# Folding a spectrum about its middle column before the back transform: two narrower matmuls out of three, 32 more vector operations

## The chip, the cores and the metric

The kernel runs on one core of a Trainium2 chip. The core has a matrix engine (PE, TensorE), a vector engine (DVE, VectorE), a scalar engine (ACT, ScalarE), a general engine (POOL, GpSimd) and a queue engine (SP, SyncE) that issues most transfers. Each engine takes its own instructions in order; semaphores tie them together. PE writes its results to PSUM, eight banks of 512 float32 columns, and DVE or ACT copy them from there.

The metric is the device time of one execution in microseconds (us).

## The reference, cut to what matters

Two mixers of the same input x (2048 tokens, 640 features) are blended by a gate:

```python
g = sigmoid((x * gate_w).sum(-1, keepdims=True))
a = _A_ref(x, A_wq, A_wk, A_wv, A_wo, A_beta)   # 32 heads, 4 causal segments of 512, with a memory between segments
b = _B_ref(x, B_w_r, B_w_i)
return g * a + (1 - g) * b

def _B_ref(x, w_r, w_i):
    X = rfft2(x.astype(float32), axes=(-2, -1))   # tokens and features
    X = X * (w_r + 1j * w_i)                      # one filter of 2048 x 321
    return irfft2(X, s=(S, D), axes=(-2, -1)).astype(bfloat16)
```

Only the second mixer, b, is touched. Its last step turns 321 complex columns k of the spectrum into 640 real features d. With real part Yr and imaginary part Yi (already back in tokens), feature d is a sum over k of Yr[k] cos(2 pi k d / 640) minus Yi[k] sin(2 pi k d / 640). The cosine part is even about d = 320 and the sine part is odd, so features d and 640 - d come from the sum and the difference of the two parts, each computed for d = 0 to 320 only.

## The kernel before, in words

**The attention** works through four segments. The logits of a segment are made in 20 units (qk_unit, L1283), 80 units in all. A unit is a group of small matmuls into four PSUM banks, an exponential on ACT (L1319) and causal masks on POOL (L1340). Products with the values, projections, feature maps on DVE (L1140, L1141) and a running memory (mem, L1193 to L1216) go with it. Segments 0 to 2 send their unnormalised outputs through DRAM (u_scr, r_scr, o_scr) and read them back for the output projection (finish_tile, L1563).

**The spectral mixer** is written in `fft` (L1422). Everything is bf16 in SBUF.

- x is folded about the middle feature on DVE or POOL (L956, L961): sums and differences with one operand read backwards, so that the forward feature transform needs narrower tables.
- F1: matmuls transform 128-token blocks and put features on the partitions (Ac).
- Sixteen groups g follow. D: six matmuls per group against tables in `big`, of 160, 161 and 321 columns, give 321 columns of cosine and of sine terms, copied to Bt (L571 on ACT or L573 on DVE). T: four matmuls with twiddle tables (tt) complete the token transform. W_mul (L1496, DVE): the filter. W_add (L1501, DVE or POOL): real and imaginary part of the filtered spectrum, written to Yt, which has two buffers. Tb: six matmuls per group with Yt as the weights, in chunks of 128, 128 and 65 columns; they put the column k on the partitions, and their results are copied to Cp.
- Db follows when all sixteen groups are in Cp. For each of 16 token blocks n2 and for cosine and sine (typ), three matmuls, one per chunk of k, add up 321 columns in one bank: 96 matmuls. The cosine part is copied to eo (ACT or DVE), and two operations on DVE (sum_Db, L1542) add and subtract it with the sine part in PSUM and write features 0 to 319 in order and 639 to 320 backwards to G. G is later read by the final matmuls (Fb) under the gate.

**The order of the work** is written out by hand as one tuple of numbers, ORDER (L633). Number // 2 is the operation in the order of recording, and the remainder picks the engine where an operation has two. `either` (L582) gives an operation to DVE or POOL in this way, and `copy_alts` (L567) to ACT or DVE. A pass over the tuple (`schedule`, L117) makes one instruction queue per engine and chooses PSUM banks; `emit` (L290) turns dependences into semaphore waits. An operation that `either` creates is marked with a lock: POOL's next instruction is made to wait for it if it runs on DVE.

Lines that the prediction uses: L561 issues nearly all matmuls (L559 those split into four), L571 and L573 the copies.

Of the kernel before, what the change touches and what calls it, by code (L numbers as in the profile page):

```python
# [8 lines left out]
ALU = mybir.AluOpType  # L9
# [3 lines left out]
P = 128  # L13
S = 2048
D = 640
# [335 lines left out]
def make_tables():  # L351
# [34 lines left out]
    IC = np.zeros((384, 322))  # L386
    IS = np.zeros((384, 322))
    IC[:KD, :KD] = ck[:, None] * np.cos(2 * pi * kd[:, None] * dd[None] / D)
    IS[:KD, :KD] = ck[:, None] * np.sin(2 * pi * kd[:, None] * dd[None] / D)
    IS[0] = 0  # L390
    IS[320] = 0
    IS[:, 320] = 0

# [34 lines left out]
    def chunks(t):  # L428
        return np.ascontiguousarray(t.reshape(3, 128, -1).transpose(1, 0, 2))
    fcat = np.concatenate([F, np.eye(128), Fp], 1)  # L430
    inv = np.concatenate([chunks(IC), chunks(IS)], 1).reshape(128, 6 * 322)
    big = np.concatenate([dtab, inv], 1)
    hmask = np.zeros((128, 5, 8, VW))
    for t in range(5):
        for r in range(128):
# [4 lines left out]
            "hmask": hmask.reshape(128, 880).astype(b)}  # L440

# [63 lines left out]
class Kern:  # L505
# [10 lines left out]
    def b(self, *key):  # L516
        v = self.bufs.get(key)
        if v is None:
            v = self.bufs[key] = Buf(str(key))
        return v  # L520
# [69 lines left out]
    def dma(self, dst, src, nbytes, r, w, prio, tr=False, name="", after=(), queue="sp"):  # L590
# [1073 lines left out]
```

## Time and profile before

| | us |
|---|---|
| median of the three runs | 240.84 (240.61 to 243.23) |
| the profiled execution's own time | 243.11 |
| its span, first to last instruction | 241.1 |
| matmuls reading Cp, first to last start | 166.0 to 204.3 |
| copies to Cp, first to last start | 61.0 to 164.0 |
| W_add, first to last start | 56.2 to 161.2 |

The profile is of one execution, 2.0 us longer than its span, and 2.3 us above the median. The clock granted to PE is 1.00 over the span. A row of a group shows the engine, the operation, what is written and read with shapes, the number of instructions, their busy time in us and the mean of one in ns; then the idle time of the engine just before them and what ended it. The durations of neighbours overlap, so means times counts can exceed the busy time. The chain is the run of work that ended last, followed back from the end.

### The profile page before, as it was taken

How to read it: one execution, taken by the hardware profiler on the slowest of the kernel's cores; microseconds unless marked ns; L12 is line 12 of the kernel's file. 1: busy time of each engine (PE TensorE's matmuls, PEld its weight loads, DVE VectorE, ACT ScalarE, POOL GpSimd, SP SyncE). 2: the span in 40 equal slices, each digit the busy share in tenths (PEclk: the TensorE clock that was granted, in tenths of full speed). 3: DMA queues.
4: the chain of work that ended last, by engine and by line, in shares of the span. 5: the costliest groups of instructions: out<-in, count | busy, mean ns of one | idle time of the engine just before them, and what ended most of it. 6: DMA issues, size and time to landing. Idle time of an engine off the chain costs nothing.

```text
span 241.1 us, 10285 instructions
## 1 busy us (share of the span) xinstructions
PE 225.2 (93%) x4347; PEld 140.6 (58%) x4361; DVE 194.7 (81%) x488; ACT 199.3 (83%) x238; POOL 158.5 (66%) x293
## 2 busy tenths in 40 slices
PE   7999996999999999999899999998998799989994
PEld 2584564776556675544566554455544466746794
DVE  0589796888999987999998999897999878645353
ACT  2199886899999999999999789998999878866830
POOL 8022137647768958648988978967995576767930
PEclk9999999999999999999999999999999999999999
DMA  7999998996978797495864882464668655842224
GB/s 167 276 358 151 277 155 182 243 229 183 225 183 183 204 204 216 100 212 132 231 207 140 225 223 44 154 193 106 200 170 239 189 147 145 113 63 75 71 73 109
DMA packets 59121, 42.18 MB, mean 175 GB/s; under 512 B 30212, under 2 KB 55364, under 8 KB 59076
## 3 DMA queue, kind: packets, MB, share of 16 engines
q1 hardware_dynamic: 57380, 40.71, 69.4%
q10 hardware_dynamic: 1696, 0.82, 1.3%
q8 instruction: 34, 0.56, 0.9%
q14 instruction: 11, 0.09, 0.1%
HBM read 23.32 MB, written 12.30 MB: 148 GB/s over the span
## 4 chain that ended last, share of the span: by engine, by line
PE 52%; DVE 18%; DMA 10%; ACT 9%; POOL 4%; SPq 3%; issue 3%; DVEq 0%
PE psum L561 50%; ACT ex L1319 6%; POOL ex L1340 3%; DVE Pt L1496 3%; DMA mT<-o_scr 3%; SPq L596 2%; PE psum L559 2%; DMA u_scr<-ub 2%; DVE Bt L573 2%; DMA dnc<-u_scr 2%; DVE G L1542 1%; DMA xsb<-in_A_x_dram 1%; DMA r<-r_scr 1%; DVE xf L956 1%; ACT et L1128 1%
## 5 line engine op out<-in xcount | busy, mean ns | idle before, releaser
L1319 ACT ACTIVATE ex<-psum 128x2048 bf16<-128x2048 f32 (+4 forms) x92 | 138.5, 1506 | 16.0 <-PE psum L561 14.4
L1340 POOL TENSOR_SCALAR_AFFINE_SELECT ex<-ex 128x256 bf16<-128x256 bf16 (+2 forms) x224 | 118.8, 553 | 28.8 <-ACT ex L1319 4.4
L561 PE MATMUL psum<-qkp 20*64 20x64 bf16 (+5 forms) x1280 | 32.7, 270 | 5.4 <-DMA qkp<-qk_scr 2.0
L561 PE MATMUL psum<-xT,wk 128*128 128x256 bf16 (+1 forms) x280 | 31.2, 273 | 0.1
L561 PE MATMUL psum<-wv,xT 128*32 128x320 bf16 (+3 forms) x400 | 29.2, 301 | 0.4 <-DVE Bt L573 0.4
L561 PE MATMUL psum<-xT,wq 128*128 128x512 bf16 (+1 forms) x121 | 27.4, 394 | 1.0 <-issue 0.5
L561 PEld LDWEIGHTS psum<-qkp 20*64 20x64 bf16 x1280 | 13.4, 103 | 22.5 <-ACT ex L1319 14.0
L1496 DVE TENSOR_TENSOR Pt<-psum,Wt 128x642 bf16<-128x642 f32 x32 | 25.2, 818 | 0.9 <-PE psum L561 0.8
L561 PEld LDWEIGHTS psum<-xT,wk 128*128 128x128 bf16 (+1 forms) x280 | 20.4, 98 | 6.0 <-issue 1.4
L559 PE MATMUL psum<-wo,oU 128*32 128x320 bf16 x480 | 21.7, 300 | 0.0
L961 POOL TENSOR_TENSOR xsb<-xf 128x320 bf16<-128x320 bf16 (+2 forms) x6 | 4.5, 745 | 24.5 <-DVE phk L1140 11.1
L561 PEld LDWEIGHTS psum<-wv,xT 128*32 128x32 bf16 (+1 forms) x400 | 14.5, 96 | 7.7 <-issue 2.2
L1171 DVE TENSOR_TENSOR va<-psum,ebx 128x320 bf16<-128x320 f32 x32 | 15.2, 485 | 4.7 <-PE psum L561 4.2
L561 PE MATMUL psum<-big,Cp 128*128 128x321 bf16 (+1 forms) x96 | 17.8, 302 | 1.1 <-DVE ot L573 0.7
L573 DVE CAST ot<-psum 128x320 bf16<-128x320 f32 x22 | 10.4, 490 | 9.8 <-PE psum L559 7.0
L561 PE MATMUL psum<-big,Ac 128*128 128x321 bf16 (+2 forms) x96 | 18.2, 257 | 0.1
L561 PE MATMUL psum<-ex,va 128*32 128x64 bf16 (+3 forms) x576 | 17.6, 257 | 0.7 <-DVE mem L1216 0.4
L561 PE MATMUL psum<-tt,Yt 128*128 128x256 bf16 (+1 forms) x96 | 17.0, 276 | 0.5 <-DVE va L1171 0.2
L561 PEld LDWEIGHTS psum<-ex,va 128*32 128x32 bf16 x576 | 10.8, 96 | 10.1 <-POOL ex L1340 2.5
L1542 DVE TENSOR_TENSOR G<-eo,psum 128x320 bf16<-128x320 f32 x32 | 14.9, 477 | 1.3 <-PE psum L561 1.1
L1501 POOL TENSOR_TENSOR Yt<-Pt 128x321 bf16<-128x321 bf16 x17 | 12.4, 731 | 5.3 <-DVE phq L1140 2.4
L1128 ACT ACTIVATE et<-qu 128x512 bf16<-128x512 bf16 x25 | 15.2, 625 | 0.3 <-DVE qu L573 0.2
(98 smaller groups left out, 388.1 us busy)
## 6 DMA issues: line engine op xcount, KB each, us to landing
qkp<-qk_scr SPq DMA_DIRECT2D x28, 160.0 KB
tt<-tab_tt SPq DMA_DIRECT2D x8, 512.0 KB, 4.0
qk_scr<-qu SPq DMA_DIRECT2D x12, 256.0 KB, 3.2
u_scr<-ub SPq DMA_DIRECT2D x12, 256.0 KB, 3.7
xsb<-in_A_x_dram SPq DMA_DIRECT2D x8, 320.0 KB, 6.8
oU<-u_scr SPq DMA_DIRECT2D x15, 128.0 KB, 4.3
out_dram<-ot SPq DMA_DIRECT2D x12, 160.0 KB
Wt<-in_B_w_r_dram SPq DMA_DIRECT2D x16, 80.2 KB, 2.8
```

Of the source, the lines that this page charges most:

```text
L559: h = e.matmul(dst, wt, r_, start=st, stop=sp_, **{**kw, "tile_position": (0, q), "skip_group_check": True})
L561: h = e.matmul(o_, l_, r_, start=st, stop=sp_, **kw)
L573: alts["dve"] = (lambda e: e.tensor_copy(dst(), src()), 67 + 1.04 * n, 68.0)
L596: return e.dma_start(d_, s_)
L961: self.either(lambda e, dst=dst, src=src, d0=d0, n=n, op=op: e.tensor_tensor(xs.ap(o + dst, [D, 2], [1, n]), xf.ap(src + d0, [321, 2], [1, ...
L1128: self.one("act", lambda e: e.activation(et.ap(0, [1, L]), qsl(), ACT.Exp), L, [qb], [b("et", pi_)], late, fix=95, name="phi_exp")
L1171: self.one("dve", lambda e: e.tensor_tensor(va.ap(i * H * VW + h0 * VW, [VW, nh], [1, DH]), self.ps(bank, 0, [DH, nh], [1, DH]), self.ebx. ...
L1319: self.one("act", lambda e, d=d, q=q: e.activation(self.ex.ap(*d), self.ps(bank, *q), ACT.Exp, scale=SC), n, [bank], [self.exb(s, 2 * pr + ...
L1340: self.one("pool", lambda e: e.affine_select(self.ex.ap(e0 + d0, [1280, 4], [1, n], np_=np_), self.ex.ap(e0 + s0, [1280, 4], [1, n], np_=np_),
L1496: self.one("dve", lambda e, ri=ri, Pt=Pt, Wt=Wt, wo_=wo_, bank=bank: e.tensor_tensor(Pt.ap(ri * 322, [644, 2], [1, KD]), self.ps(bank, 0, ...
L1501: fn = lambda e, r=r, a0=a0, a1=a1, op=op, Pt=Pt, Yt=Yt: e.tensor_tensor(Yt.ap(r * 322, [1, KD]), Pt.ap(a0 * 322, [1, KD]), Pt.ap(a1 * 322 ...
L1542: self.one("dve", lambda e, q=q, n2=n2, bank=bank, eo=eo: e.tensor_tensor(self.G.ap(n2 * D + 639 * q, [1 - 2 * q, 320]), eo.ap(q, [1, 320] ...
```

## The change

Column 320 - k has the cosine of column k up to a sign: cos(2 pi (320 - k) d / 640) = (-1)^d cos(2 pi k d / 640), and likewise for the sine with the sign reversed. So even features need only the sums, and odd features only the differences (for the sine the other way round), of columns k and 320 - k.

- **Z_fold** (new, two per group, 32 in all): Zt takes the sums of Yt[k] and Yt[320 - k] for k = 0 to 160 and the differences for k = 0 to 159, real and imaginary part in one operation. It runs on DVE or POOL as ORDER says.
- Tb reads Zt in place of Yt, in the same chunks of 128, 128 and 65.
- Db: the first chunk holds only sums, the last only differences, so they need only the columns of one parity of d. The three matmuls of a bank are 161, 321 and 160 columns wide for the cosine and 160, 321 and 161 for the sine; before, all were 321. The results stand in the bank with the even and the odd features apart.
- sum_Db reads the two halves and writes every second element of G, again in two operations.
- Yt has one buffer, Zt two. The tables in `big` shrink from 3220 to 2576 columns, and so does their load.
- ORDER is another tuple. The 80 logit units come in the same sequence as before. Z_fold is on DVE 22 times and on POOL 10 times; W_add is on DVE 28 times and on POOL 4 times, before 15 and 17.

```diff
-        self.big = T("big", [P, 1288 + 6 * 322])
+        self.big = T("big", [P, 2576])
...
-        self.Yt = [T(f"Yt{i}", [P, 2 * 322]) for i in range(2)]
+        self.Yt = T("Yt", [P, 2 * 322])
+        self.Zt = [T(f"Zt{i}", [P, 2 * 322]) for i in range(2)]
...
+DB_PARTS = (((0, 0, 161, 0), (1, 0, KD, 162), (2, 161, 160, 484)), ((0, 161, 160, 644), (1, 0, KD, 804), (2, 0, 161, 1126)))
...
+            for q, (n, op) in enumerate(((161, ALU.add), (160, ALU.subtract))):
+                self.either(lambda e, q=q, n=n, op=op, Yt=Yt, Zt=Zt: e.tensor_tensor(
+                    Zt.ap(161 * q, [322, 2], [1, n]), Yt.ap(0, [322, 2], [1, n]), Yt.ap(320, [322, 2], [-1, n]), op), 2 * n,
+                    Yb, [b("Zt", g % 2, q)], prio2, after=self.after_q0(("Zt", g % 2, q)), name="Z_fold")
...
-                            return (self.ps(bank, (c % 2) * 256, [1, 256], np_=kc), Yt.ap(r * 322 + c * P, [1, kc]), tt.ap(to + 512 + r * 256, [1, 256]),
+                            return (self.ps(bank, (c % 2) * 256, [1, 256], np_=kc), Zt.ap(r * 322 + c * P, [1, kc]), tt.ap(to + 512 + r * 256, [1, 256]),
...
-                for c in range(3):
-                    kc = 65 if c == 2 else P
-
-                    def th(c=c, typ=typ, kc=kc, n2=n2, bank=bank):
-                        return (self.ps(bank, 0, [1, KD]), self.Cp.ap(c * 4096 + typ * 2048 + n2 * P, [1, P], np_=kc),
-                                big.ap(1288 + (typ * 3 + c) * 322, [1, KD], np_=kc), c == 0, c == 2, {})
+                for n_, (c, c0, n, tc) in enumerate(DB_PARTS[typ]):
+                    def th(c=c, c0=c0, n=n, tc=tc, n_=n_, typ=typ, kc=65 if c == 2 else P, n2=n2, bank=bank):
+                        return (self.ps(bank, c0, [1, n]), self.Cp.ap(c * 4096 + typ * 2048 + n2 * P, [1, P], np_=kc),
+                                big.ap(1288 + tc, [1, n], np_=kc), n_ == 0, n_ == 2, {"skip_group_check": True})
...
-                        self.G.ap(n2 * D + 639 * q, [1 - 2 * q, 320]), eo.ap(q, [1, 320]), self.ps(bank, q, [1, 320]),
+                        self.G.ap(n2 * D + 638 * q, [1, 2], [2 - 4 * q, 160]), eo.ap(q, [161 - q, 2], [1, 160]), self.ps(bank, q, [161 - q, 2], [1, 160]),
                         ALU.subtract if q else ALU.add), 320, [bank, eb], [b("G", n2, q)], prio, name="sum_Db", after=acb)
```

More of the change, by code (lines that the diff above doesn't have):

```diff
@@ L385, in make_tables, with folded @@
     dd = np.arange(KD)
[L386 to L389, printed above, removed]
+    IC = ck[:, None] * np.cos(2 * pi * kd[:, None] * kd[None] / D)
+    IS = ck[:, None] * np.sin(2 * pi * kd[:, None] * kd[None] / D)
+    IC[160] *= 0.5
+    IS[160] *= 0.5
     IS[0] = 0
-    IS[320] = 0
     IS[:, 320] = 0
+    def folded(M, odd):
+        Z = np.zeros((KD, KD))
+        Z[:161, 161 if odd else 0:KD if odd else 161] = M[:161, odd::2]
+        Z[161:, 0 if odd else 161:161 if odd else KD] = M[:160, 1 - odd::2]
+        return Z
+    ZC, ZS = folded(IC, 0), folded(IS, 1)
     T = np.zeros((16, 128, 4, 128))
@@ L426, in make_tables, with part @@
                     putp(0, 0, eo, c), putp(1, 0, eo, -s), putp(0, 1, eo, -s), putp(1, 1, eo, -c)
-    def chunks(t):
-        return np.ascontiguousarray(t.reshape(3, 128, -1).transpose(1, 0, 2))
+    def part(Z, c, c0, c1):
+        q = np.zeros((128, (c1 - c0 + 1) // 2 * 2))
+        rows = Z[128 * c:128 * c + 128, c0:c1]
+        q[:len(rows), :c1 - c0] = rows
+        return q
     fcat = np.concatenate([F, np.eye(128), Fp], 1)
-    inv = np.concatenate([chunks(IC), chunks(IS)], 1).reshape(128, 6 * 322)
+    inv = np.concatenate([part((ZC, ZS)[typ], c, c0, c0 + n) for typ in range(2) for c, c0, n, _ in DB_PARTS[typ]], 1)
     big = np.concatenate([dtab, inv], 1)
@@ L837, in after_mid @@
         return ([b("tt", i) for i in range(self.NT)] + [b("Wt", i, r, h) for i in range(2) for r in range(2) for h in range(2)] +
-                [b("Bt", i, r) for i in range(2) for r in range(2)] + [b("Yt", i, r) for i in range(2) for r in range(2)] +
+                [b("Bt", i, r) for i in range(2) for r in range(2)] + [b("Yt", r) for r in range(2)] + [b("Zt", i, q) for i in range(2) for q in range(2)] +
                 [b("Pt", i, r, q) for i in range(2) for r in range(2) for q in range(2)])
@@ L909, in loads @@
                      P * 2 * D * 2, [], [self.b("xsb", q)], 1.0 + 0.2 * q, name="ld_x")
-        self.dma(lambda: self.big.ap(0, [1, 3220]), lambda: dap(self.tab["big"].ap(), 0, [3220, P], [1, 3220]),
-                 P * 6440, [], [self.b("big")], 5.0, name="ld_big")
+        self.dma(lambda: self.big.ap(0, [1, 2576]), lambda: dap(self.tab["big"].ap(), 0, [2576, P], [1, 2576]),
+                 P * 5152, [], [self.b("big")], 5.0, name="ld_big")
         self.dma(lambda: self.hm.ap(0, [1, 880]), lambda: dap(self.tab["hmask"].ap(), 0, [880, P], [1, 880]),
@@ L1483, in fft @@
                            r=[bank], w=[Bb], after=self.after_q0(("Bt", g % 2, typ)), prio=prio, name="ev_D")
-            Pt, Yt = self.Pt[g % 2], self.Yt[g % 2]
+            Pt, Yt, Zt = self.Pt[g % 2], self.Yt, self.Zt[g % 2]
             Pb = [[b("Pt", g % 2, ri, r) for r in range(2)] for ri in range(2)]
-            Yb = [b("Yt", g % 2, i) for i in range(2)]
+            Yb = [b("Yt", i) for i in range(2)]
             for ri in range(2):
@@ L1502, in fft @@
                     Yt.ap(r * 322, [1, KD]), Pt.ap(a0 * 322, [1, KD]), Pt.ap(a1 * 322, [1, KD]), op)
-                self.either(fn, KD, [Pb[0][r], Pb[1][1 - r]], [Yb[r]], prio2, after=self.after_q0(("Yt", g % 2, r)), name="W_add")
+                self.either(fn, KD, [Pb[0][r], Pb[1][1 - r]], [Yb[r]], prio2, after=self.after_q0(("Yt", r)), name="W_add")
+            for q, (n, op) in enumerate(((161, ALU.add), (160, ALU.subtract))):
+                self.either(lambda e, q=q, n=n, op=op, Yt=Yt, Zt=Zt: e.tensor_tensor(
+                    Zt.ap(161 * q, [322, 2], [1, n]), Yt.ap(0, [322, 2], [1, n]), Yt.ap(320, [322, 2], [-1, n]), op), 2 * n,
+                    Yb, [b("Zt", g % 2, q)], prio2, after=self.after_q0(("Zt", g % 2, q)), name="Z_fold")
+            Zb = [b("Zt", g % 2, q) for q in range(2)]
             for cs in ((0, 1), (2,)):
@@ L1511, in fft, with th @@
                     for r in range(2):
-                        def th(c=c, r=r, kc=kc, Yt=Yt, tt=tt, to=to, bank=bank):
-                            return (self.ps(bank, (c % 2) * 256, [1, 256], np_=kc), Yt.ap(r * 322 + c * P, [1, kc]), tt.ap(to + 512 + r * 256, [1, 256]),
+                        def th(c=c, r=r, kc=kc, Zt=Zt, tt=tt, to=to, bank=bank):
+                            return (self.ps(bank, (c % 2) * 256, [1, 256], np_=kc), Zt.ap(r * 322 + c * P, [1, kc]), tt.ap(to + 512 + r * 256, [1, 256]),
                                     r == 0, r == 1, {})
                         items.append((th, 256))
-                    self.mms(items, Yb + [b("tt", ti), bank], [], prio3, name="Tb", mode=0)
+                    self.mms(items, Zb + [b("tt", ti), bank], [], prio3, name="Tb", mode=0)
                 n_, np_, c0 = len(cs), (65 if cs[0] == 2 else P), cs[0]
@@ L1527, in fft @@
                 bank = Bank(1, "gen")
-                for c in range(3):
-                    kc = 65 if c == 2 else P
-                    def th(c=c, typ=typ, kc=kc, n2=n2, bank=bank):
-                        return (self.ps(bank, 0, [1, KD]), self.Cp.ap(c * 4096 + typ * 2048 + n2 * P, [1, P], np_=kc),
-                                big.ap(1288 + (typ * 3 + c) * 322, [1, KD], np_=kc), c == 0, c == 2, {})
-                    self.mms([(th, KD)], cpb + [b("big"), bank], [], prio, name="Db", mode=0)
+                for n_, (c, c0, n, tc) in enumerate(DB_PARTS[typ]):
+                    def th(c=c, c0=c0, n=n, tc=tc, n_=n_, typ=typ, kc=65 if c == 2 else P, n2=n2, bank=bank):
+                        return (self.ps(bank, c0, [1, n]), self.Cp.ap(c * 4096 + typ * 2048 + n2 * P, [1, P], np_=kc),
+                                big.ap(1288 + tc, [1, n], np_=kc), n_ == 0, n_ == 2, {"skip_group_check": True})
+                    self.mms([(th, n)], cpb + [b("big"), bank], [], prio, name="Db", mode=0)
                 eo, eb = self.eo[n2 % 3], b("eo", n2 % 3)
```

197 rows, old and new, of the table ORDER are left out of this document.

## The prediction

> **What bounds the kernel now.** I read the engine totals first, then the same engines by stretch of the span, then the groups of the rows that the change touches, then the waits and the chain.
>
> ```profile
> PE 225.2 (93%) x4347; PEld 140.6 (58%) x4361; DVE 194.7 (81%) x488; ACT 199.3 (83%) x238; POOL 158.5 (66%) x293
> ```
>
> By the totals TensorE (PE) is the bound and the change takes work from it. But a total is an average over stages, so I cut the span at the exponentials of the logit units (ACT, L1319): the 10th starts at 53.05 us, the 55th at 163.49 us and the 60th at 174.20 us. Busy us of each engine in these stretches:
>
> ```profile
> core 0: us, PE busy (x) PEld busy (x) DVE busy (x) ACT busy (x) POOL busy (x), PEclk, DMA share, GB/s
> ...
> 52.60:163.00 110.40, 106.60 (x1874) 63.52 (x1885) 102.93 (x248) 103.90 (x114) 85.96 (x164) 1.00 0.71 181
> 163.00:173.70 10.70, 9.75 (x200) 6.17 (x192) 9.05 (x27) 9.69 (x12) 8.58 (x19) 1.00 0.59 161
> ...
> 173.70:241.10 67.40, 60.34 (x1569) 40.27 (x1568) 45.54 (x117) 47.82 (x56) 43.59 (x76) 1.00 0.51 126
> ```
>
> In the middle stretch three engines are nearly full together: PE 97%, DVE 93%, ACT 94%. All spectrum groups (L1470 to L1520) run there, and the added instructions go there. The back transform (Db, the matmuls that read Cp) runs from 166.0 to 204.3 us, almost all in the last stretch, where DVE is 68% busy. So the change takes from PE late and gives to DVE in the middle.
>
> [...]
>
> The groups of the rows that change or resemble what is added (busy us, mean ns of one, idle before):
>
> ```profile
> L561 PE MATMUL psum<-big,Cp 128*128 128x321 bf16 x64 | 13.8, 303 | 1.1 <-DVE ot L573 0.7 <-DVE mem L1216 0.2
> L561 PE MATMUL psum<-big,Ac 128*128 128x321 bf16 x32 | 9.4, 302 | 0.0
> L561 PE MATMUL psum<-big,Ac 128*128 128x161 bf16 x32 | 7.4, 235 | 0.1
> L561 PE MATMUL psum<-big,Ac 128*128 128x160 bf16 x32 | 7.3, 234 | 0.0
> L1501 POOL TENSOR_TENSOR Yt<-Pt 128x321 bf16<-128x321 bf16 x17 | 12.4, 731 | 5.3 <-DVE phq L1140 2.4 <-DVE phq L1141 0.9 <-DVE dn L1208 0.7
> L1501 DVE TENSOR_TENSOR Yt<-Pt 128x321 bf16<-128x321 bf16 x15 | 5.4, 374 | 0.1
> L961 DVE TENSOR_TENSOR xsb<-xf 128x322 bf16<-128x322 bf16 x7 | 2.3, 325 | 0.0
> ```
>
> **The change part by part.**
>
> *Removed from PE.* Of each three Db matmuls of 321 columns, two become 160 or 161 columns wide. The forward matmuls from Ac have exactly these widths: 302 ns against 235 and 234, so 67.5 ns less each. 64 such matmuls: **4.3 us less on PE**. The instructions stay 96, the weight loads too. Before 173.7 us the new order does 30 Db matmuls where the old did 27, and keeps 6 more Tb matmuls for that stretch, so nothing is gained there. After it, 69 become 66: about 3.4 us less of PE's 60.3. In the middle stretch PE has the same matmuls but for 2 more D and 6 fewer Tb: nothing.
>
> *Added to DVE and POOL.* 32 Z_fold operations (16 groups, sum and difference, 322 and 320 elements). The written order puts 22 on DVE and 10 on POOL. The same order moves W_add: from 15 on DVE and 17 on POOL to 28 and 4. The fold's nearest row is the fold of x (L961): two bf16 inputs, one read backwards, an odd offset, 322 elements: 325 ns on DVE, and 730 ns for its like on POOL. In the middle stretch (same logit units in both orders) DVE gets 20 Z_fold x 325 = 6.5 and 13 W_add x 374 = 4.9, and loses three copies to Bt (518 each, 1.6), one phi pair (0.8), one copy to Cp (0.7) and three small gate operations (0.5), and gains one projection copy (0.7): **8.5 us more by durations**. Durations of neighbours overlap: in the chain three folds in a row took 0.80 us, 0.27 each, not 0.33. Over the stretch the old order's DVE durations by these rows sum to 117 us and show as 102.9 busy, a factor 0.88. So 7.5 us more, 110.4 us of DVE in a stretch that lasts 110.4. It can only keep its length if DVE never waits. How full can DVE get? Its five fullest ten-microsecond windows in this stretch show 9.87, 9.67, 9.57, 9.55 and 9.54, mean 96.4%; at that, the stretch takes 114.5 us, **4.1 longer**. Bounds: the fullest window's 98.7% gives 111.9 (1.5 longer), today's 93.2% gives 118.4 (8.0 longer). I take the mean of the fullest windows, since PE and ACT get no new work and stop being what DVE waits for. From 163.0 to 173.7 us DVE gets 1.8 us more by the same rows, with 1.65 us of idle: **0.5 longer** (0 to 1.5).
>
> *POOL* loses 13 x 731 = 9.5 and gains 10 x 740 = 7.4: 2 us less, with 24 us idle in the stretch: nothing.
>
> *The last stretch.* Which part of the 3.4 us counts? The chain there:
>
> ```profile
> 80 pieces in order of time: start us, us, what
> ...
> 182.25 4.47 DMA u_scr<-ub
> ...
> 186.74 3.74 DMA dnc<-u_scr
> ...
> 206.27 6.15 DMA mT<-o_scr
> ...
> 228.03 9.62 PE psum L561 x276
> ```
>
> From 182 to 219 us it runs mostly through DMAs, DVE and the masks on POOL, and after 206 us no Db is left. PE holds about 4.5 us of the chain between 174 and 206. Bounds: 0 and 3.4; I take **1.5 shorter**, since some other PE work can slip forward into the freed time. The sums of G (L1542) now write every second element. The copy to Bt writes so too and takes 518 ns for 322 elements where ot takes 490 for 320; 32 x 28 ns = 0.9 us on an engine that is 68% busy: nothing, 0.9 if the cover is gone.
>
> *Small edits.* Yt has one buffer instead of two: the next W_add waits for both folds. Groups come 110/16 = 6.9 us apart, so nothing; it costs up to 0.7 us where the order has two groups close together. One more link (0.33 on DVE, 0.74 on POOL) lies between W_add and Tb; at the end the last Cp copy starts at 164.0 and the first Db at 166.0, which hides it. The table load shrinks by a fifth; it is issued at 42.7 and first read at 51.5 us: nothing. SP issues the same number of transfers.
>
> *Sum.* 4.1 + 0.5 - 1.5 = **3.1 us longer**. The profiled execution took 243.11 us (span 241.1 and 2.0 around it) and would become 246.2. It is 2.3 above the median of 240.84, so on the median's scale I predict **243.9 us**. Extremes: 1.5 + 0 - 3.4 = -1.9 and 8.0 + 1.5 + 0.9 + 0.7 = +11.1.
>
> **Rivals.**
>
> *PE is the bound throughout, DVE has slack (faster).* For it: 97% against 93% in the middle, and of the 5.7 us that the waits list for DVE from 55 to 165 us, 5.5 are for PE. Then the middle keeps its length and the whole 3.4 us counts: 237.4; with half of it 239.1. Against it: the middle's PE work is not reduced, and DVE would have to be 100% busy. It decides where the 7.5 us shrink to about 4, so that DVE stays below 97%: an added operation at 0.12 us. Chance 0.2.
>
> *The lock between DVE and POOL (slower still).* POOL already waits for two-input DVE work:
>
> ```profile
> POOL ex L1340 <- DVE phk L1141: 3.0, 7, 0.7
> ...
> POOL ex L1340 <- DVE Yt L1501: 2.5, 4, 0.9
> ```
>
> The DVE W_add itself ranges from 309 to 603 ns. If each of the 33 more such DVE operations met a mask (0.29 us, the spread), DVE would lose up to 9.6 us more, and masks would come late to the product with the values. It decides from about a third of them, 3.2 us: 247 to 250. Against it: the mean is 374, only 65 ns above the least. Chance 0.12. [...]
>
> [...] L961's form is so close that I give it 0.08.
>
> **How the numbers follow.** My forecast, 241.3 to 247.5, has 0.60; the faster rival 0.20 (237.4 to 240.5), the lock 0.12, the slow fold 0.08. A change under 1% (2.4 us, 238.4 to 243.2) is about what a measurement here can't tell from none. Of the forecast's chance 0.22 lies below 243.2, of the faster rival's 0.06 above 238.4. So faster 0.14, same 0.28, slower 0.58. The range 238.2 to 248.0 leaves out about 0.12 below and 0.08 above.
>
> **What would show it.** Right: from the 10th to the 55th exponential 112 to 118 us instead of 110.4, DVE at 96% or more there; Db rows of 160 and 161 columns near 235 ns; Zt rows near 325 ns on DVE and 740 on POOL; from the 60th exponential to the end 1 to 2 us less. Wrong: a middle stretch of 110 us or less with DVE busy under 108, which would mean that copies and waits overlap more than I count, or a last stretch shorter by all of 3.4 us.

## The result

The changed kernel takes **249.56 us** (median of four executions, 249.02 to 252.03) against 240.9 for the kernel before on the same chip: ratio 1.0327, 95% interval 1.0264 to 1.0391. Slower, as the forecast said, but by 8.6 us instead of 3.1, and beyond the end of the range (248.0).

The granted TensorE clock of one and the same kernel differs between executions (0.966 to 0.985 in the four of the changed kernel, 0.971 to 1.000 in the ten of e10 below), so where it matters I give times "at a whole clock", which are those of executions with a mean granted clock of 0.998 or more.

The totals and the clock row on the page of the changed kernel, and below them the clock row of the kernel before (a row has 40 equal slices of the span, 6.3 us each in the changed kernel; a digit is the granted clock in tenths):

```profile
span 250.2 us, 10318 instructions
...
PE 228.8 (91%) x4361; PEld 142.3 (57%) x4361; DVE 201.9 (81%) x522; ACT 198.4 (79%) x238; POOL 155.8 (62%) x291
...
PEclk9999999999997799999979999999999599999999
```
```profile
PEclk9999999999999999999999999999999999999999
```

TensorE (PE) was given less to do and is busy 3.6 us longer than before (225.2); 2.5 us of this are like for like, since the trace of the changed kernel holds 14 matmul records more, 1.1 us of busy time, at the same 4361 weight loads. The clock row tells why: before it was 9 in every slice, now it falls in three places. A matmul takes longer there: the Tb matmuls of 128x256 take 421 ns on the mean from 78.1 to 85 us and 275 from 85 to 92.

I cut the span at the same exponentials as in the forecast, the 10th and the 55th. In the changed kernel they start at 51.68 and 171.38 us:

```profile
core 0: us, PE busy (x) PEld busy (x) DVE busy (x) ACT busy (x) POOL busy (x), PEclk, DMA share, GB/s
51.68:171.38 119.70, 111.23 (x1867) 65.30 (x1865) 107.25 (x272) 105.06 (x117) 83.51 (x158) 0.96 0.72 167
```

The stretch takes 119.7 us instead of 110.4. This looks like the forecast at twice its size, but VectorE (DVE) is only 107.25/119.70 = 90% busy, less full than before (93%). So something else ended the waits. Subtracting the start times of the same exponentials, after minus before, shows where. An ordinary table, worked out from the start times of the ACT rows:

| exponential | before, us | after minus before |
|---|---|---|
| 10 | 53.05 | -1.37 |
| 19 | 75.82 | -1.02 |
| 22 | 83.52 | +5.24 |
| 35 | 116.30 | +5.32 |
| 37 | 120.43 | +8.47 |
| 55 | 163.49 | +7.89 |

I call this difference the lateness of an exponential. An engine that is too full would, as I took it, lose a little at every unit. Here the lateness is nearly flat over 9, 13 and 18 units, and jumps twice, by 6.3 and by 3.2 us. What happens at the jumps, busy time by window, same columns as above; the last two rows are the kernel before, for comparison with the first two:

```profile
76.00:78.00 2.00, 0.00 (x0) 0.00 (x0) 1.03 (x3) 1.17 (x2) 1.93 (x4) 1.00 1.24 171
78.00:85.00 7.00, 5.28 (x38) 2.91 (x39) 2.55 (x7) 3.20 (x4) 1.55 (x4) 0.51 0.39 100
85.00:92.00 7.00, 7.00 (x112) 4.38 (x110) 6.28 (x18) 5.54 (x7) 4.66 (x8) 1.00 0.77 189
...
122.00:124.50 2.50, 0.46 (x6) 0.19 (x4) 1.35 (x4) 1.43 (x3) 2.20 (x5) 1.00 1.07 147
124.50:131.00 6.50, 6.33 (x93) 3.82 (x98) 4.72 (x15) 4.50 (x4) 3.13 (x8) 0.74 0.85 229
...
192.00:194.00 2.00, 0.32 (x3) 0.11 (x2) 1.59 (x5) 1.39 (x1) 1.03 (x3) 1.00 0.90 284
194.00:201.00 7.00, 6.70 (x84) 2.62 (x87) 5.65 (x15) 3.42 (x2) 4.61 (x8) 0.52 0.84 196
```
```profile
76.00:78.00 2.00, 1.91 (x46) 1.13 (x43) 2.00 (x8) 2.00 (x2) 1.96 (x4) 1.00 0.50 95
78.00:85.00 7.00, 6.95 (x117) 4.58 (x117) 6.89 (x17) 6.81 (x7) 6.69 (x14) 1.00 0.72 200
```

Three times TensorE does next to nothing for 2 to 2.5 us, and each time its clock is about half for part of the following 7 us (in windows of half a microsecond it reads 0.50 from about 78.2 to 85.0 us, from 126.0 to 129.4 and from 194.3 to 201.1): 38 matmuls between 78 and 85 us, 112 in the next 7. The timeline of TensorE names what it waited for (start, length, line, tiles, count, and in brackets the idle time before it and its releaser):

```profile
75.08 0.73 PE L573 MATMUL psum<-ex,va 128*32 128x512 bf16 x24
78.11 0.68 PE L573 MATMUL psum<-va,pkn 128*128 128x176 bf16 x4 [2.30 <-DMA pkn<-phk]
80.40 0.70 PE L573 MATMUL psum<-va,pkn 128*128 128x154 bf16 x4 [1.61 <-DMA pkn<-phk]
```

These are the memory update matmuls of a segment (mupd in the code, the 7th and 8th of 15, counted from 0). They read pkn, which a transposing DMA (pkT, L606, on SP's queue) fills from phk. The list of TensorE's waits has pkn in front, and the chain that ended last names it too (second fence). In the kernel before, no wait for pkn is in that list:

```profile
PE psum L573 <- DMA pkn<-phk: 6.0, 3, 2.3
PE psum L573 <- DVE eo L585: 1.7, 1, 1.7
```
```profile
74.00 6.35 DMA pkn<-phk
...
117.24 7.16 DMA pkn<-phk
```

At 192 us it is another wait of the same kind: TensorE waits 1.7 us for an eviction (eo, L585) that stands in VectorE's queue behind five multiplications of oU (L1600), the last of which waits 1.0 us for a DMA load of oU.

In the kernel before, SP issues the fourth transpose (counted from 0) at 64.62 us, and now at 72.06, with one short transfer between it and the fifth at 74.00. None of these waits is for the fold. They lie in the written order, where transfers and the matmuls that read them stand otherwise to each other.

### The profile page after: what moved, and what is told of

It reads as the page before. It is cut to its first block, busy times and chain, and to the rows that moved or that the text cites. A ratio compares the mean times of both kernels' runs of the same rounds, so it can differ in the third digit from the quotient of the medians.

```text
span 250.2 us, 10318 instructions
## 1 busy us (share of the span) xinstructions
PE 228.8 (91%) x4361; PEld 142.3 (57%) x4361; DVE 201.9 (81%) x522; ACT 198.4 (79%) x238; POOL 155.8 (62%) x291
## 4 chain that ended last, share of the span: by engine, by line
PE 47%; DVE 20%; DMA 16%; ACT 6%; SPq 5%; issue 3%; POOL 1%; DVEq 0%; POOLq 0%
PE psum L573 39%; PE psum L571 7%; DMA pkn<-phk 5%; ACT ex L1333 5%; DVE Pt L1510 4%; DMA qkp<-qk_scr 3%; DMA xT<-in_A_x_dram 3%; SPq L608 3%; SPq L606 3%; DMA fcat<-tab_fcat 2%; DMA oU<-u_scr 2%; DVE Cp L585 2%; DVE Bt L585 1%; DVE ub L585 1%; DVE Yt L1515 1%
## 5 line engine op out<-in xcount | busy, mean ns | idle before, releaser
L573 PE MATMUL psum<-qkp 20*64 20x64 bf16 (+5 forms) x1280 | 33.6, 276 | 5.1 <-ACT ex L1333 1.7
L573 PE MATMUL psum<-xT,wk 128*128 128x256 bf16 (+1 forms) x280 | 34.4, 277 | 0.0
L573 PE MATMUL psum<-xT,wq 128*128 128x512 bf16 (+1 forms) x135 | 32.5, 388 | 0.5 <-DMA xT<-in_A_x_dram 0.5
L571 PE MATMUL psum<-wo,oU 128*32 128x320 bf16 x480 | 22.6, 313 | 0.0
L573 PE MATMUL psum<-big,Cp 128*128 128x321 bf16 (+4 forms) x96 | 15.7, 266 | 3.1 <-DVE eo L585 1.7
L573 PE MATMUL psum<-tt,Zt 128*128 128x256 bf16 (+1 forms) x96 | 17.8, 284 | 0.4 <-DVE Pt L1510 0.3
L585 DVE CAST ot<-psum 128x320 bf16<-128x320 f32 x20 | 9.6, 491 | 10.4 <-PE psum L571 8.0
L573 PE MATMUL psum<-big,Ac 128*128 128x161 bf16 (+2 forms) x96 | 17.2, 257 | 0.1
L1559 DVE TENSOR_TENSOR G<-eo,psum 128x320 bf16<-128x320 f32 x32 | 16.0, 506 | 1.5 <-PE psum L573 0.7
L571 PEld LDWEIGHTS psum<-wo,oU 128*32 128x32 bf16 x480 | 12.5, 100 | 5.0 <-issue 1.6
L975 POOL TENSOR_TENSOR xsb<-xf 128x320 bf16<-128x320 bf16 (+1 forms) x4 | 3.0, 741 | 19.8 <-DVE xsb L975 16.7
```

The lines of the kernel that those rows point to most:

```text
L571: h = e.matmul(dst, wt, r_, start=st, stop=sp_, **{**kw, "tile_position": (0, q), "skip_group_check": True})
L573: h = e.matmul(o_, l_, r_, start=st, stop=sp_, **kw)
L585: alts["dve"] = (lambda e: e.tensor_copy(dst(), src()), 67 + 1.04 * n, 68.0)
L975: self.either(lambda e, dst=dst, src=src, d0=d0, n=n, op=op: e.tensor_tensor(xs.ap(o + dst, [D, 2], [1, n]), xf.ap(src + d0, [321, 2], [1, ...
L1559: self.one("dve", lambda e, q=q, n2=n2, bank=bank, eo=eo: e.tensor_tensor(self.G.ap(n2 * D + 638 * q, [1, 2], [2 - 4 * q, 160]), eo.ap(q, ...
```

## The experiments

Theories: **order** (the written order lets TensorE reach some matmuls before their transfers have landed; it idles, and its clock is then halved), **vector work** (the forecast: VectorE is full in the middle), and **addresses** (the tiles behind Zt lie 64 bytes higher, and the transposes became slower for that: their median from issue to landing, when the data are in place, went from 4.5 to 6.4 us). In the diffs that move entries of the written order I put names in the place of the numbers: "mupd8" is the 8th memory update, pkT a transpose into pkn, xT one of x, qk a logit unit, pvf a product with the values, and D, T and Tb are the steps of the spectral mixer. Every ratio is to the kernel before on the same chip.

### Addresses, and the order by itself

```diff
 e1 (the changed kernel)
-        self.Zt = [T(f"Zt{i}", [P, 2 * 322]) for i in range(2)]
+        self.Zp = T("Zp", [P, 1300])
+        self.Zt = [T(f"Zt{i}", [P, 2 * 322], at=self.Zp.off + i * 1312) for i in range(2)]
 e2 (the kernel before)
+        self.gap = T("gap", [P, 32])
         self.wq = T("wq", [P, 5 * D])
 e3 (the kernel before)
-    ORDER = (the order of before)
+    ORDER = (the order of the changed kernel, without its 32 Z_fold)
```

> The changed kernel with the two Zt buffers packed 32 bytes apart instead of 64, so that every SBUF tile behind them (weights, xT, qu, phk, pkn, qkp, ub, mem and all others) lies at the address it had before the change, 64 bytes lower. Nothing else differs. Addresses theory (transfers to and from tiles shifted by 64 bytes take longer; nine transposes to pkn took 6.4 us to land in the median instead of 4.5, TensorE idled for them and lost its clock): the transposes land in about 4.5 us, the granted clock stays at 1.00, and the time falls by 6 to 10 us to 239 to 243. Order theory (the new written order asks for pkn too early): nothing changes, 249 to 250. Vector work theory (the forecast): nothing changes, 249 to 250.

> The kernel before with 64 unused bytes put in front of wq, so that all tiles from wq on lie 64 bytes higher, as in the changed kernel. Addresses theory: the transposes to pkn land in about 6.4 us and the time rises by 4 to 10 us to 245 to 251, with stalls of TensorE on pkn or qkp. Order and vector work theories: no change, 240 to 242.

> The kernel before, at its own addresses and with its own arithmetic (Db 321 columns wide, no fold), in the order of the changed kernel with the 32 fold operations left out: W_add 28 times on VectorE and 4 on GpSimd. Order theory: TensorE idles for pkn as in the changed kernel, 245 to 250. Addresses theory: 240 to 244. Vector work theory: 13 more W_add on VectorE cost about 4 us of it, 1 to 3 us more in time, 242 to 244.

| | median us | ratio to before | pkn landing, median us |
|---|---|---|---|
| e1 changed kernel, old addresses | 251.83 (243.41 to 252.59) | | 5.5 |
| e2 before, addresses shifted | 241.6 | 0.9994 (0.9941 to 1.0048) | 4.9 |
| e3 before, new order, no fold | 250.43 (248.34 to 251.41) | 1.0398 (1.0317 to 1.0479) | 6.0 |

The addresses fall as the cause: shifting them in the kernel before costs nothing, and putting them back keeps the loss in three of four executions, with waits of 4.2 us for pkn in the one traced. The fourth took 243.41 us at a clock of 0.986, so how much is paid varies between executions, which e19 shows again below. The old arithmetic in the new order is as slow as the changed kernel, without one fold. Its waits and its clock row:

```profile
PE psum L561 <- DMA pkn<-phk: 5.5, 3, 2.2
```
```profile
PEclk9999999999997699999869999999999999999999
```

So **the order costs 9.6 us by itself** (250.43 against the 240.8 that the ratio gives). "Order" here takes in which engine does an operation, with 13 more W_add on VectorE. The fold in the same order gives -0.9 us (249.56 against 250.43), which the overlapping intervals of the two ratios do not tell from nothing.

### Is it the transfers?

```diff
 e5 (the kernel before): SP's queue in the changed kernel's sequence, the four other queues untouched
 e12 (the kernel before), SP's queue
- pkT4 ... (8 transfers) ... xT10 pkT5
+ ... (8 transfers) ... xT10 pkT4 pkT5
 e7 (the changed kernel), SP's queue
- pkT3 pad5 ... (10 transfers) ... W9 pkT4 pad4 pkT5
+ pkT3 pad5 pkT4 ... (10 transfers) ... W9 pad4 pkT5
- tt4 st_u4 pkT8
+ pkT8 tt4 st_u4
```

> The kernel before, with its arithmetic and its order on the four computing engines, but SP's queue in the changed kernel's sequence. Transfer theory (the transposes into pkn stand later in SP's queue, and TensorE idles for them and is then slowed): the fourth transpose is again issued next to the fifth, TensorE waits over 1 us for pkn at one or two places, and the time is 245 to 251. If it is the sequence on the computing engines that counts: 240 to 242.5, with under 1 us of waits for pkn.

> The kernel before with one entry of SP's queue moved: the fourth transpose into pkn is issued right before the fifth, as in the changed kernel, some 6 us later than it was. Idle theory: TensorE waits 1.5 to 2.5 us for pkn near 74 to 79 us, its granted clock then shows 0.50 for 4 to 7 us, and the time is 243 to 247. If the half clock has another cause: 240.5 to 242 at a clock of 1.00, or at most the wait itself.

> The changed kernel with two of SP's entries moved up: the fourth transpose into pkn to where its data are ready (some 8 us earlier), and the eighth ahead of the 512 KB table load and the u_scr store that stood in front of it. Transfer theory: the waits for pkn fall from 6 us to under 2 us, the first two stretches of half clock go, the third (near 192 us) stays; 241 to 246. Vector work theory (the forecast: VectorE is full in the middle stretch): 248 to 250, with the same lateness of the exponentials as in the changed kernel.

e5 took 262.5 us (ratio 1.0775, 1.0666 to 1.0883), far above both expectations. It waits 6.8 us for pkn, but also 3.9 for xsb and 3.1 for masks, which stand with other transfers in the old order. A queue taken out of one order does not fit another; of the transposes alone it tells nothing.

e12 took 240.81 (0.9958, 0.9919 to 0.9997), with a whole clock and no wait for pkn. My expectation was wrong: a late fourth transpose does no harm here. There both transposes are issued from 70.28 us on, and TensorE comes to the first group at 75.43, 5.2 us behind its transpose, and to the second at 75.75, 4.1 behind its own (71.64). In the changed kernel it is ready for both from 75.81 on, 3.8 and 1.8 us behind the issues at 72.06 and 74.00. From issue to landing, the changed kernel first and e12 second:

```profile
DMA to landing us min/median/max: 5.9/6.4/7.2
```
```profile
DMA to landing us min/median/max: 3.1/3.7/4.1
```

**What counted here is the distance between the transfer and its reader, set against the time to land**, not the place of the transfer: by estimate, with the 5.9 to 7.2 us of the changed kernel set against its 5.2 and 4.1, e12 would have waited too. Why the transposes take 6 us in one order and 4 in another I did not settle, so this half of the cause stays open.

e7 took 247.24 (1.0265, 1.0200 to 1.0329): less than the changed kernel, more than the 241 to 246 expected, since one wait and the idle place near 188 us were left. Where it waits it pays: its lateness (after minus before, as in the table) goes from -1.63 at the 19th exponential to +2.06 at the 22nd, 3.7 us for this one wait:

```profile
PE psum L573 <- DMA pkn<-phk: 2.1, 1, 2.1
```

### Taking the idle places away

```diff
 e8 (the changed kernel), the queues of TensorE and VectorE
- memrd3 pvf5 mupd7 mupd8 Tb8 qk16 ... D33 proj120 D34 D35
+ memrd3 pvf5 Tb8 qk16 ... D33 mupd7 proj120 D34 D35 mupd8
- mupd13 qk32 memrd12 T17 ... mupd14 ... memrd14 ... T19
+ qk32 memrd12 T17 ... memrd14 mupd13 ... T19 mupd14
  (and the five m_add that read them, behind them)
 e10: e7 and e8, and in VectorE's queue
- normal2 normal7 sum_Db20 ev_Db8 sum_Db18 gate_ops26 sum_Db21 sum_Db19 normal9 normal8 normal6 normal5
+ normal2 sum_Db20 ev_Db8 sum_Db18 gate_ops26 sum_Db21 sum_Db19 normal7 normal8 normal6 normal5 normal9
 e14: e7, the new place of the normal, and of e8 only this
- mupd7 mupd8 Tb8 qk16 ... pvf7
+ mupd7 Tb8 qk16 ... pvf7 mupd8
```

> The changed kernel with all transfers where they are, and the four waiting groups of memory update matmuls (with the VectorE additions that read them) moved one to two logit units back in the queues of TensorE and VectorE. If what costs the time is that TensorE idles for the transposes, and not that these land late: waits for pkn under 1 us, no half clock before 190 us, 241 to 245. If late transposes also delay something else, or VectorE sets the pace: 247 to 250.

> Both of these together, and the five VectorE multiplications that wait for oU moved behind six instructions that TensorE waits for. Idle theory: no stretch of half clock is left; the exponentials stand level with the kernel before or up to 1 us ahead at the 56th, and the fold's arithmetic shows undisturbed: 237 to 241. Vector work theory: the middle stretch still takes about 4 us longer than before, 243 to 246.

> The changed kernel with a smaller repair: both transposes earlier, of the update matmuls only the eighth group moved back, by one logit unit, with its two additions, and the five multiplications moved back. Idle theory: no wait for pkn over 0.5 us and no half clock; without the 2.5 us that the repaired kernel lost near 118 to 125 us, 238 to 241.5. If the fold's load on VectorE takes what TensorE saves: 241 to 243.

| | median us | ratio to before | at a whole clock, us |
|---|---|---|---|
| e8 matmuls later | 245.3 (243.29 to 247.6) | 1.0144 (1.0057 to 1.0230) | none of 4 |
| e10 all three | 243.97 (241.78 to 250.27) | 1.0046 (0.9992 to 1.0100) | 242.19, 5 of 10 |
| e14 repaired | 241.16 (240.18 to 244.2) | 0.9996 (0.9957 to 1.0036) | 240.96, 8 of 10 |

e8 moves no transfer, only the readers, and has no half clock before 187 us: it is TensorE's idling that costs, as expected, though the time is 0.3 us above the range given. e10 missed its 237 to 241: its median and its middle stretch, 4.8 us longer than before, are what the vector work theory said. Its partner e11, below, tells the two apart. e14 brings the whole loss back. Its page:

```profile
span 238.4 us, 10304 instructions
...
PE 222.4 (93%) x4347; PEld 139.8 (59%) x4361; DVE 200.9 (84%) x522; ACT 198.1 (83%) x238; POOL 158.1 (66%) x291
...
PEclk9999999999999999999999999999999999999999
```

It does the same arithmetic as the changed kernel, and its VectorE is busy as long (200.9 against 201.9). TensorE is busy 6.4 us less by these rows, some 5 us without the 14 records that only the changed kernel's trace has, though it runs the same matmuls, because none of them runs at half clock. Between e14 and the changed kernel lie a few places in three queues and 8.4 us. It does not beat the kernel before.

### What the fold is worth where TensorE does not idle

```diff
 e11: the order of e10, e18: the order of e14, each with the old arithmetic (the 32 Z_fold left out of the order)
 e13: the order of e10
-                self.either(lambda e, q=q, n=n, op=op, Yt=Yt, Zt=Zt: e.tensor_tensor(
-                    Zt.ap(161 * q, [322, 2], [1, n]), Yt.ap(0, [322, 2], [1, n]), Yt.ap(320, [322, 2], [-1, n]), op), 2 * n,
+                def halves(e, q=q, n=n, op=op, Yt=Yt, Zt=Zt):
+                    k = 2 if e is self.nc.vector else 1
+                    for p0 in range(0, P, P // k):
+                        h = e.tensor_tensor(Zt.ap(161 * q, [322, 2], [1, n], p0=p0, np_=P // k), ...
+                    return h
```

> The repaired order of the run before (transposes earlier, update matmuls and multiplications later) with the old arithmetic: the folds left out, the back transform over all 321 columns again. Against the repaired kernel with the fold (242.2 where its clock stayed whole) this has some 4.3 us more TensorE work and some 7.5 us less VectorE work. Forecast's theory (VectorE sets the pace in the middle): 237 to 239. TensorE sets the pace: 244.5 to 247. Neither, the written order does: 240.5 to 243.5.

> The order of e14 with the old arithmetic (no folds, the back transform over 321 columns). If the fold brings what it brought in the other repaired order: 243 to 244.5, and the middle stretch within 0.7 us of e14's 112.73. If it brings nothing in a clean order: 240 to 242. If it costs (forecast): 237 to 239.

> The repaired kernel with each of the 22 folds on VectorE issued as two instructions, partitions 0 to 63 and 64 to 127: the same result, and about twice the time of a fold, so 22 times 0.35, some 7.7 us more VectorE work, most of it in the middle stretch. Forecast's theory (VectorE full there): 5 to 8 us longer than the repaired kernel at a whole clock, 247 to 250. VectorE has room: at most 2 us longer, 242 to 244.

| order | old arithmetic | with the fold |
|---|---|---|
| as written | e3: 250.43 | the changed kernel: 249.56 |
| e10 | e11: 245.05 (4) | 242.19 (5, whole clock) |
| e14 | e18: 244.61 (11, whole clock) | 240.96 (8, whole clock) |

The fold brings 2.9 and 3.7 us at a whole clock. By the ratios to the kernel before, 1.0046 (e10) against 1.0132 (e11, 1.0071 to 1.0193) and 0.9996 (e14) against 1.0074 (e18, 1.0028 to 1.0120), it is about 2 us in both orders. So the fold alone is worth some 2 to 4 us where TensorE does not idle.

The same ratios say something else: without the fold both repaired orders are still 0.7 to 1.3% slower than the kernel before, 2 to 3 us, with no wait for pkn and a whole clock. That part of the order's 9.6 us has another cause, which no run here names.

The middle stretch with it (e10, e14) and without it (e11, e18), and with the folds in halves (e13), each between its own 10th and 55th exponential, in the order e10, e11, e14, e18, e13:

```profile
50.15:165.34 115.19, 107.34 (x1855) 63.38 (x1865) 107.45 (x272) 104.74 (x117) 83.14 (x158) 1.00 0.73 173
```
```profile
50.46:165.28 114.82, 107.82 (x1857) 63.46 (x1868) 103.70 (x250) 104.92 (x118) 75.18 (x148) 1.00 0.72 173
```
```profile
50.58:163.31 112.73, 107.08 (x1855) 63.23 (x1865) 107.33 (x272) 104.85 (x117) 83.28 (x158) 1.00 0.73 177
```
```profile
51.22:165.44 114.22, 107.81 (x1857) 63.31 (x1868) 104.08 (x250) 105.43 (x117) 75.22 (x148) 1.00 0.70 174
```
```profile
50.90:172.10 121.20, 108.20 (x1855) 62.99 (x1865) 115.69 (x292) 105.40 (x117) 82.77 (x158) 1.00 0.68 164
```

The fold adds 3.75 and 3.25 us of busy VectorE, and the stretch gets 0.4 us longer in one order and 1.5 shorter in the other. These are single executions, and those of e18 at a whole clock lie 4.9 us apart, so I read both as "no longer". This is not what the forecast said. But e13 (251.66 us, 1.0374, 1.0296 to 1.0453) is what it said, one step further on: another 8.2 us of VectorE make the stretch 6.0 us longer, at a whole clock and 95.5% full. TensorE there waits 3.4 us for Bt and only 1.7 for Zt itself, so it is the fuller queue more than the longer way from Yt to Tb. **In these orders VectorE had room for the fold and no room for a second one.** The room is small: e14 is 107.33/112.73 = 95.2% full. In a stretch as short as the 110.4 us of the kernel before, the same work would by estimate fill 107.33/110.4 = 97%, and no run here reaches that.

### The fold in the old order

```diff
 e15 (the changed kernel), the order of before with the folds behind each group's two W_add
+ W_add W_add Z_fold Z_fold
  (W_add on the old engines: 17 on GpSimd; two groups of Tb behind their folds)
```

> The changed arithmetic in the order of the kernel before: every instruction at its old place on its old engine, the 32 folds put in behind the additions they read (22 on VectorE, 10 on GpSimd, as in the changed kernel), and two groups of back transform matmuls moved behind the fold they now need. If the written order makes the loss and the fold brings 2 to 3 us, as it did in the repaired order (245.05 without it, 242.2 with it): 238 to 240.5, the granted clock whole, VectorE some 4 us busier in the middle stretch. If the fold costs what the forecast said, 4 us in the middle against 1.5 won later: 243 to 245. If GpSimd, which keeps its 17 additions here, holds the folds up: 241 to 246, with waits of VectorE or TensorE for it.

260.94 us (1.0808, 1.0756 to 1.0860). The third case came, and worse: GpSimd (POOL) has its 17 W_add, the masks and 10 folds, and TensorE waits for it directly:

```profile
PE psum L573 <- POOL ex L1355: 5.9, 9, 2.1
PE psum L573 <- POOL Zt L1520: 4.2, 3, 2.2
```

So the old order has no room for the fold as I placed it. The order written with the change has most W_add on VectorE; it had room for the fold and three idle places.

### One wait, and one try more

```diff
 e19: e14 with mupd8 and its two m_add back at their place
- mupd7 Tb8 qk16 ... pvf7 mupd8
+ mupd7 mupd8 Tb8 qk16 ... pvf7
 e17: e14, queues of TensorE and VectorE
- memrd5 T9
+ T9 memrd5
- mem_den5 mem_rec5 W_mul9
+ W_mul9 mem_den5 mem_rec5
```

> The repaired kernel e14 with the eighth group of update matmuls and its two additions back at their place, one logit unit earlier, so that TensorE meets one transpose that has not landed. Idle theory: one wait for pkn of 1.5 to 2.2 us, 0.50 of the clock for 3 to 5 us behind it, no other half clock; 2.5 to 4 us longer than e14, 243.5 to 245. If a wait costs only itself: 242.5 to 243.2.

> The repaired kernel e14 with the ninth transform group and the multiplication that frees its PSUM bank moved ahead of one memory read and its denominator, since TensorE waited 1.1 us for that bank near 77 us. If that lateness is the order's: 1 us shorter than e14, 239.3 to 240.5. If VectorE's load sets it: as e14, 240.5 to 242.

e19 took 239.56 to 248.12 us in ten executions, median 244.15. Three had a whole clock (239.56, 240.58, 242.70); in the seven others it was 0.972 to 0.993 and the median 245.93. The same program pays in some executions and not in others. The profiled one waited:

```profile
70.00:77.00 7.00, 5.25 (x98) 3.34 (x97) 6.32 (x15) 6.47 (x8) 4.67 (x9) 1.00 1.08 212
77.00:79.00 2.00, 0.40 (x6) 0.40 (x6) 0.00 (x0) 0.00 (x0) 2.00 (x5) 1.00 0.72 192
79.00:84.00 5.00, 4.78 (x53) 2.53 (x51) 3.15 (x8) 3.40 (x5) 1.79 (x4) 0.66 0.47 132
```

Its wait for pkn was 3.0 us and its lateness rose by 4.6 from the 19th to the 22nd exponential, so 1.6 us come on top, which I put down to the half clock. The same sum gives 6.3 - 3.9 = 2.4 for the first idle place of the changed kernel (3.9 are the two waits of 2.30 and 1.61), 3.2 - 2.1 = 1.1 for the second (2.1 is what they leave of the 6.0) and 3.7 - 2.1 = 1.6 for e7. **In these four places a wait of 2 to 4 us cost 1.1 to 2.4 us more than itself.** I had expected one place; this execution was slowed near 188 and 218 us too, which the moved wait does not explain.

e17 took 243.81 us (1.0080, 1.0029 to 1.0132), 241.23 at a whole clock (5 of 12): no gain over e14. Its lateness still grows by 0.9 us from the 19th to the 21st exponential, as in e14, so the bank that I blamed is not the cause. The 2.3 us that e14 loses in the middle against the kernel before stay unexplained; they are not the fold's, since e18 without it loses 3.8.

## Why the prediction was wrong

**What held.** The sign, by luck: the loss came from a term that the sum does not have, and the fold alone makes the kernel faster. The prices of single operations held too. The Db matmuls: 321 columns take 302 ns and 160 or 161 columns 234 to 240 in e14 (forecast 302 and 235), so 64 matmuls save some 4.2 us. The fold's rate: 370 and 339 ns in e10 where L961's 325 was taken, 764 and 761 on GpSimd in the changed kernel for 740. The fold reads one operand backwards; W_add on VectorE, which reads none so, took 340 ns in e10. So the slow fold (0.08) did not come. The lock rival was half right and cost nothing seen here: in e14 the masks wait more for VectorE, 4.7 us for Yt (2.5 before) and 3.0 for Zt, but W_add on VectorE did not slow down (374 ns before, 344 in e14), and TensorE's waits for masks went from 0.6 to 0.4 us. These waits of the masks are on semaphores that the kernel itself writes for its locked operations, so they show that order and nothing beyond it.

**The step that failed: "SP issues the same number of transfers", taken as enough, which put the new order at nothing.** The number was the same and the places were not. I compared what each engine does in each stretch, and never how far each transfer stands ahead of the matmul that reads it. The order shows this before any run: twelve transfers stand between the third and the fourth pkn transpose, where six stood, and one between the fourth and the fifth, where nine stood, while the readers stay at the same logit unit. That term measured 9.6 us in e3, larger than everything in the sum; 5.5 us of it are TensorE's waits for pkn, and the lateness in e3 jumps by 6.2 and 4.6 us where they stand.

**A second step that failed: "at that, the stretch takes 114.5 us, 4.1 longer".** It took 119.7, for the reason above, and the term itself was too large.
- *What VectorE gets:* 7.5 us forecast, 107.25 - 102.97 = 4.3 measured in the changed kernel. The fold's share is 3.75 (e10 against e11), though its 22 rows sum to 7.8. I scaled added durations by the mean factor of the whole stretch, 0.88; here it was 0.48. Part of it is that other rows shrink (in the middle stretch, phq at L1155 from 362 to 318 ns, rc from 650 to 256); the rest was not settled.
- *What that does:* by the forecast's own rule, 96.4% as the most that VectorE can be filled, 107.25 us need 111.3, 0.8 us longer than 110.4 and not 4.1. The limit is real, and near the place that I gave it (e13 at 95.5%). Only the load was put too high.

**The last stretch.** 1.5 us forecast of at most 3.4. From the forecast's boundary, the exponential at 174.20 us in the kernel before (the 61st when the others are counted as above), to the end of the span e10 takes 64.7 and e11 67.0 us, e14 64.2 and e18 67.3: **2.3 and 3.1 us less**, one execution of each. In these two pairs, with a whole clock, most of the PE saving counted. In the changed kernel the idle place at 192 us ate the saving.

**The rivals.** "PE is the bound throughout, VectorE has slack" (0.20, 237.4 to 240.5) is close to what the fold does alone, some 2 to 4 us less. Its condition, "where the 7.5 us shrink to about 4", was met with 4.3. It was right about the arithmetic and wrong about the kernel, since the order came with it.

## What to carry over

A change that comes with a new written order is two changes: run the old arithmetic in the new order before you argue about the arithmetic. When comparing two orders, list for each transfer how long before its first reader it is issued, and set that beside its time to land in the trace; where less than the landing time was left here (3.8 and 1.8 us against 5.9 to 7.2), TensorE idled. In the four places measured here TensorE's idling was charged again by half as much or more. A lateness that grew in jumps pointed to waits here; that one growing at every unit points to a full engine is my assumption, which no run here showed.

## What the runs showed that I had not expected

- **The clock halved after gaps of 2 us, and the length of the gap alone does not decide it.** In the changed kernel it was 1.00 while TensorE idled from 76 to 78 us, 0.51 on the mean from 78 to 85 and 1.00 after. The three halved stretches of that execution lasted 6.8, 3.4 and 6.8 us, the one behind the wait of e19 near 78 us 3.4. Gaps of 2.0 to 2.5 us were enough here, and gaps of 1.3 us (e7, at 186 us) and 1.2 us (e1, at 191 us) were followed by a half clock too (the clock rows show 8 and 5 in the two slices from 184 us of e7 and from 188 us of e1). The kernel before idled for 1.95 us at 36.7 us and kept a whole clock, 1.00 from 36.5 to 45 us. What decides it stays open.
- **A fold over half the partitions took as long as one over all.** Over 64 partitions the two took 349 and 357 ns (e13), over 128 partitions 370 and 339 (e10).
- **An address shift of 64 bytes did nothing** (e2, 0.9994), though the transposes' landing times differ by 2 us between orders.
